# Fewer zero matmuls, an earlier first theta, sinks after the product, and one set of PSUM banks in a fused attention and mixer kernel

## The chip, the cores and the metric

The kernel runs on one core of one Trainium2 chip. The metric is the device time of one execution, in microseconds (us). Before the change three runs took 607.32, 607.62 and 608.21 us; the median is 607.62.

## The reference

The program is one fused block for batch 2, 768 positions and 512 channels, all in float32:

```
a   = softmax(where(is_sink | in_window, q k^T / 8, -1e9)) v   # 8 heads of 64, 4 sinks, window 128
x   = a as (2, 768, 512)
th  = x @ w_theta                                              # (512, 512)
y   = w_tok_r @ (x * cos th) + w_tok_i @ (x * sin th)          # mixes the 768 positions
u   = x + y;  x2 = u + relu(u @ w_ch)
m   = x2 + real(fft2(x2));  out = m + relu(norm(m) @ w_ch1) @ w_ch2
```

The kernel multiplies in a reduced float32 format and regains the precision by splitting an operand into a high and a low part: a product is three matmuls, high x high weight, high x low weight, low x high weight.

## The kernel before

The attention loop (`attn_banded`) walks through 12 tiles (n = 0 to 11, six of 128 positions for each of two batches), each in four steps s; 48 steps, and some more in which the rest drains. In the even steps `score_mms` issues a group of four score matmuls (one for each head) into the four banks of a ring, VectorE (L515) masks each and takes its minimum, and ScalarE (L519) takes the exponential; the second group of a tile fills the banks in reverse order. "S(n, 0)" and "S(n, 1)" below are the two score groups of tile n; S(2, 1), for one, belongs to step 10. One step later `turn` transposes the exponentials (`tp`), and ScalarE or VectorE copies them out. Six steps after a tile's first step `av` multiplies them with v into the one bank `oa`; the next step transposes the result back (`av_turn`), and VectorE normalizes it (L610 in the profile).

The 16 sink columns have their own product: `psk` is transposed into `oa`, copied to `pst`, and `av_sink` multiplies it with `vs` as the first writer of the accumulation in `oa`. `theta_gen` transposes the normalized tile (`tp<-ident,t`), splits it (ScalarE copies it to xT, GpSimd makes the high part, L808, and the low part, L211), and issues 12 matmuls into the bank `th` in the order high, high, low for each quarter of the channels.

The theta of tile u starts at step `first(u)` = 4u + 5 + max(4, 12 - u): step 17 for u = 0, 20 for u = 1, and 4u + 9 from u = 8 on. In steps 1 to 16 two matmuls of a tile of zeros go to the bank `th` after each step's scores (L651); they compute nothing that is used. The weights of theta come as 64-bit numbers and are converted on ScalarE and VectorE (`pump`, L279 to L291) in the steps of `THS`, and split one step later (L206, L211).

After attention `rest` runs `y_gen(0)`, the mixing over positions: for each block j of 128 positions the cosine and the sine product (`trig_mul`, L842 in the profile) are split and multiplied with converted weights into six banks: 24 matmuls of 512 columns and 24 of 256. j = 0 to 5 follow each other; cosine first, sine second, about 4.2 us of TensorE each.

Order: Tile's scheduler places the instructions of each engine by their dependencies and its own time model, so the code's order is only one input. The PSUM banks are eight tiles. One (`bank`) is held for the whole program; the other seven come from a pool of the attention part (`psa`), and after its end again seven from a second pool (`ps`) for the same memory. Every engine works its own queue in order.

## Time and profile before

| | us |
|---|---|
| median of three runs | 607.62 |
| profiled execution | 607.02 |
| its span, first to last instruction | 605.2 |
| TensorE (PE) busy | 588.4 |
| ScalarE (ACT), VectorE (DVE), GpSimd (POOL) busy | 345.4, 335.2, 332.8 |

The span is 1.8 us shorter than the profiled execution, and that execution is 0.6 us below the median. In a timeline row the columns are start, duration, engine, line, operation, out<-in and count; square brackets hold the idle time before and what ended it. Matmuls overlap, so a group's cost on TensorE is the distance from its start to the start of the next, not its duration. A float32 matmul of zeros or scores stands in the trace as two records.

### The profile page before, as it was taken

The page shows a single profiled execution, that of the slowest core. Times are in us where ns is not written, and L with a number is a line of the kernel's source. Part 1 is how long each engine was busy: PE and PEld are TensorE (multiplying, and loading weights), DVE is VectorE, ACT ScalarE, POOL GpSimd, SP SyncE. Part 2 cuts the span into 40 slices and gives each one's busy share as a digit, 9 for nine tenths or more (in the row PEclk, how much of TensorE's full clock was granted, in tenths as well). Part 3 has the DMA queues.
Part 4 walks back from the last instruction along what each step waited for, and adds up shares of the span by engine and source line. Part 5 has one row for each costly group of instructions (what it writes and reads, how often), then busy time and mean ns, then how long its engine had stood idle before and what let it go on. Part 6 is the DMA issues. An engine that isn't in the chain of part 4 may idle for free.

```text
span 605.2 us, 9829 instructions
## 1 busy us (share of the span) xinstructions
PE 588.4 (97%) x3606; PEld 513.1 (85%) x3606; DVE 335.2 (55%) x685; ACT 345.4 (57%) x774; POOL 332.8 (55%) x281
## 2 busy tenths in 40 slices
PE   8999999998999999989999999999999999999995
PEld 6777777786888899968999999998998899998994
DVE  5767657756999678983566765465334211121112
ACT  5776666667774564556678784437447444344340
POOL 1113664658885552517654746759757565665650
PEclk9999999999999999999999999999999999999998
DMA  7942333310334323710067650100001000010001
GB/s 227 343 137 67 110 122 105 89 36 0 105 106 137 116 70 105 209 35 2 2 179 206 195 152 0 53 2 0 2 0 54 1 0 1 2 52 1 0 2 58
DMA packets 23338, 46.63 MB, mean 77 GB/s; under 512 B 2512, under 2 KB 9552, under 8 KB 23280
## 3 DMA queue, kind: packets, MB, share of 16 engines
q1 hardware_dynamic: 22032, 43.74, 23.2%
q0 software_dynamic: 1248, 2.17, 1.2%
q8 instruction: 30, 0.49, 0.3%
q14 instruction: 28, 0.23, 0.1%
HBM read 42.75 MB, written 3.15 MB: 76 GB/s over the span
## 4 chain that ended last, share of the span: by engine, by line
PE 83%; DVE 8%; ACT 5%; issue 1%; POOL 1%; DMA 0%; ACTq 0%; DVEq 0%; POOLq 0%
PE pc L221 26%; PE acc L221 22%; PE s L221 9%; PE bank L221 8%; PE oa L221 3%; PE th L221 3%; PE tp L226 3%; PE sc L221 2%; PE th L651 2%; PE s L226 2%; ACT p L519 1%; ACT t L206 1%; POOL t L211 1%; PE bank L391 1%; DVE t L211 1%
## 5 line engine op out<-in xcount | busy, mean ns | idle before, releaser
L211 POOL TENSOR_TENSOR t<-t 128x512 fp32r<-128x512 f32 x151 | 202.7, 1363 | 166.9 <-ACT t L206 138.1
L221 PE MATMUL acc<-t 128*128 128x512 f32 x648 | 178.7, 394 | 0.0
L206 ACT ACTIVATE t<-t 128x512 fp32r<-128x512 f32 x172 | 102.1, 626 | 70.8 <-PE acc L221 26.5
L221 PEld LDWEIGHTS acc<-t 128*128 128x128 f32 x648 | 116.5, 188 | 17.9
L221 PE MATMUL pc<-t 128*128 128x384 f32 (+1 forms) x672 | 124.9, 314 | 1.0 <-POOL t L211 0.6
L221 PEld LDWEIGHTS pc<-t 128*128 128x128 f32 x672 | 113.8, 188 | 10.9 <-POOL t L211 0.8
L1156 DVE SCALAR_TENSOR_TENSOR t<-pc,t 128x384 fp32r<-128x384 f32 x64 | 35.6, 557 | 124.2 <-ACT t L1155 122.9
L221 PE MATMUL s<-t 128*128 128x256 f32 (+3 forms) x492 | 70.5, 286 | 1.6 <-DVE st L1076 0.8
L221 PE MATMUL pc<-uh,t 128*128 128x384 f32 x256 | 70.6, 337 | 0.0
L221 PEld LDWEIGHTS s<-t 128*128 128x128 f32 x492 | 65.9, 190 | 4.9 <-DVE st L1076 1.0
L211 POOL TENSOR_TENSOR t<-xT,t 128x512 fp32r<-128x512 f32 x39 | 52.8, 1372 | 28.2 <-ACT t L206 27.9
L1155 ACT ACTIVATE t<-pc 128x384 fp32r<-128x384 f32 x64 | 31.3, 489 | 60.8 <-PE pc L221 58.0
L221 PE MATMUL bank<-t 128*128 128x512 f32 x216 | 65.1, 398 | 0.9 <-DVE t L211 0.9
L279 ACT ACTIVATE raw<-raw 128x512 f32<-128x512 f32 x58 | 39.1, 678 | 14.8 <-DMA raw<-in_w_ch_dram 12.6
L221 PEld LDWEIGHTS pc<-uh,t 128*128 128x128 f32 x256 | 46.2, 188 | 0.8
L221 PEld LDWEIGHTS bank<-t 128*128 128x128 f32 x216 | 38.7, 188 | 7.8 <-DVE t L211 1.8
L221 PE MATMUL pc<-ul,t 128*128 128x384 f32 x128 | 43.0, 336 | 0.6 <-DVE ul L211 0.6
L519 ACT ACTIVATE p<-sc,nb 128x272 f32<-128x272 f32 (+1 forms) x72 | 32.8, 464 | 12.8 <-DVE nb L515 12.8
L221 PE MATMUL th<-t 128*128 128x512 f32 x132 | 35.9, 408 | 0.7 <-POOL t L211 0.7
L823 POOL TENSOR_SCALAR t<-t 128x512 f32<-128x512 f32 x12 | 25.4, 2117 | 16.2 <-ACT t L822 16.1
L515 DVE CUSTOM_DVE_ANT_0 sc<-sc,m 128x272 f32<-128x272 f32 (+1 forms) x72 | 28.6, 446 | 8.9 <-PE sc L221 8.9
L206 ACT ACTIVATE t<-xT 128x512 fp32r<-128x512 f32 x36 | 21.0, 625 | 19.1 <-PE acc L221 7.4
(144 smaller groups left out, 842.1 us busy)
## 6 DMA issues: line engine op xcount, KB each, us to landing
raw<-in_w_ch_dram SPq DMA_DIRECT2D x36, 512.0 KB, 3.8
kst<-in_k_dram SPq DMA_DIRECT2D x12, 256.0 KB, 4.1
t<-in_v_dram SPq DMA_DIRECT2D x12, 256.0 KB, 5.1
raw<-in_w_tok_rT_dram SPq DMA_DIRECT2D x6, 512.0 KB, 3.6
raw<-in_w_tok_iT_dram SPq DMA_DIRECT2D x6, 512.0 KB, 3.6
out_dram<-t SPq DMA_DIRECT2D x12, 256.0 KB, 2.1
t<-in_q_dram SPq DMA_DIRECT2D x11, 256.0 KB, 4.7
raw<-in_w_theta_dram SPq DMA_DIRECT2D x4, 512.0 KB, 6.9
```

Source lines behind the costliest of these rows:

```text
L206: return nc.scalar.activation(o, i, AF.Copy).ins
L211: e.tensor_tensor(o, x, hi.bitcast(F32), op=ALU.subtract)
L221: i = self.nc.tensor.matmul(o, lhsT=lhsT, rhs=rhs, start=start, stop=stop, skip_group_check=True).ins
L226: self.chained(self.nc.tensor.transpose(o, x, ident).ins)
L279: nc.scalar.activation(hf, hf, AF.Copy, scale=2.0 ** -112)
L391: nc.tensor.matmul(self.bank[:, 0:256], lhsT=z[:, 0:128], rhs=z, start=k == 0, stop=False, skip_group_check=True)
L515: nc.vector.tensor_tensor_reduce(out=sc[:, 0:wd], in0=sc[:, 0:wd], in1=mask, op0=ALU.add, op1=ALU.min, scale=-0.125, scalar=3.0e38, accum_ ...
L519: self.last_exp = nc.scalar.activation(p[:, h, 0:wd], sc[:, 0:wd], AF.Exp, bias=nb[:, h:h + 1], scale=-1.0, accum_out=sm[:, h:h + 1]).ins
L651: i = nc.tensor.matmul(self.zth[:, 0:256], lhsT=self.zz[:, 0:128], rhs=self.zz, start=s == 1, stop=False, skip_group_check=True,).ins
L823: nc.gpsimd.tensor_scalar(km, ph, MAGIC, MAGIC, op0=ALU.add, op1=ALU.subtract)
L1155: nc.scalar.activation(hh, hp, AF.Relu)
L1156: self.hl = nc.vector.scalar_tensor_tensor(hl, in0=hp, scalar=0.0, in1=hh.bitcast(F32), op0=ALU.max, op1=ALU.subtract).ins
```

## The change

The zeros stop after step 6 (`ZE`). `T0` falls from 12 to 10, which starts theta two steps earlier up to tile 6, and one for tile 7; two of the four theta weights are converted one and two steps earlier. In `theta_gen` the eight matmuls with the high part come first and the four with the low part last. The sink product is issued after the product with v and no longer opens the accumulation. The eight PSUM banks are allocated once, and the rings of both parts of the program name the same tiles.

```diff
@@ constants
-T0 = 12
+T0 = 10
+ZE = 7
-THS = (6, 9, 12, 15)
+THS = (6, 9, 11, 13)
@@ class _Ring
-    def __init__(self, pool, n, shape, dt, name, also=()):
-        self.tiles = [*also, *(pool.tile(shape, dt, name=f"{name}{i}") for i in range(n))]
+    def __init__(self, pool, n=0, shape=None, dt=None, name=None):
+        self.tiles = [pool.tile(shape, dt, name=f"{name}{i}") for i in range(n)] if n else pool
@@ start
-        self.bank = ctx.enter_context(tc.tile_pool(name="bank", bufs=1, space=PSUM)).tile([128, 512], F32, name="bank")
+        banks = ctx.enter_context(tc.tile_pool(name="bank", bufs=1, space=PSUM))
+        self.banks = [banks.tile([128, 512], F32, name=n) for n in ("bank", "a0", "a1", "a2", "c0", "c1", "s0", "s1")]
+        self.bank = self.banks[0]
@@ av_sink, av
-    def av_sink(self, n):
-        b, i = self.seq[n]
-        self.oacc = self.ps_acc.next().rearrange("p (a m) -> p a m", a=4)
-        if i < 2:
-            return
-        pst = self.pt.pop((n, 4))
-        for a in range(4):
-            self.mm(self.oacc[:, a], self.vs[b][:, 2 * a:2 * a + 2].rearrange("p h d -> p (h d)"), pst, a == 0, False)
-
     def av(self, n):
         b, i = self.seq[n]
-        acc = self.oacc
+        acc = self.ps_acc.next().rearrange("p (a m) -> p a m", a=4)
...
-                        i < 2 and hp == 0 and m == parts[0][1], hp == 3 and m == parts[-1][1],
+                        hp == 0 and m == parts[0][1], i < 2 and hp == 3 and m == parts[-1][1],
...
         self.hold = self.pe
+        if i >= 2:
+            pst = self.pt.pop((n, 4))
+            for a in range(4):
+                vs = self.vs[b][:, 2 * a:2 * a + 2].rearrange("p h d -> p (h d)")
+                self.mm(acc[:, a], vs, pst, False, a == 3)
@@ attn_banded
-            if 0 < s < first(0):
+            if 0 < s < ZE:
...
-            if 0 <= g + 1 <= last and k == 3:
-                self.av_sink(g + 1)
@@ theta_gen
-        for a in range(4):
-            wh, wl = self.ws["th", a]
-            self.mm(th, hi[:, a, :], wh, a == 0, False)
-            self.mm(th, hi[:, a, :], wl, False, False)
-            self.mm(th, lo[:, a, :], wh, False, a == 3)
-            if a < 3:
+        for k in range(12):
+            a, x = (k // 2, hi) if k < 8 else (k - 8, lo)
+            self.mm(th, x[:, a, :], self.ws["th", a][k < 8 and k % 2], k == 0, k == 11)
+            if k % 3 == 2 and k < 11:
                 yield
@@ all
-            self.ps_sc = _Ring(ps, 3, [128, 512], F32, "sc", [self.bank])
-            self.ps_tp = _Ring(ps, 2, [128, 512], F32, "tp")
-            self.ps_acc = _Ring(ps, 1, [128, 512], F32, "oa")
-            self.ps_th = _Ring(ps, 1, [128, 512], F32, "th")
+            self.ps_sc = _Ring(self.banks[0:4])
+            self.ps_tp = _Ring(self.banks[4:6])
+            self.ps_acc = _Ring(self.banks[6:7])
+            self.ps_th = _Ring(self.banks[7:8])
...
-            self.ps_acc = _Ring(ps, 3, [128, 512], F32, "acc", [self.bank])
-            self.ps_pc = _Ring(ps, 2, [128, 512], F32, "pc")
-            self.ps_s = _Ring(ps, 2, [128, 512], F32, "s")
+            self.ps_acc = _Ring(self.banks[0:4])
+            self.ps_pc = _Ring(self.banks[4:6])
+            self.ps_s = _Ring(self.banks[6:8])
```

So a0 to a2 are the old `sc` and `acc`, c0 and c1 the old `tp` and `pc`, s0 the old `oa`, s1 the old `th` (numbers 68 to 74 in the rows below). The engines' orders differ from the first dropped zeros up to block j = 2 of `y_gen(0)`; after that TensorE's is the same but for the names.

First place, TensorE from the second score group of tile 3 on; `<-kst,t` are scores, `<-ident,p` transposes of exponentials, `psk` that of the sinks, `<-t 64x128` the product with v, `pst` that of the sinks, `<-z` the zeros, `<-ident,t` into c_72 the transposes of the first theta. Before:

```order
L221 MATMUL sc_205<-kst,t 128x288
L221 MATMUL sc_204<-kst,t 128x288
L221 MATMUL sc_203<-kst,t 128x288
L221 MATMUL bank<-kst,t 128x288
L221 MATMUL oa_208<-pst_171,t 128x128 x4
L221 MATMUL oa_208<-t 64x128 x16
L651 MATMUL th_209<-z 128x256 x2
L226 MATMUL tp_207<-ident,p_186 128x128 x4
L651 MATMUL th_209<-z 128x256 x2
L226 MATMUL tp_206<-ident,p_186 128x128 x4
```

And now:

```order
L222 MATMUL a_70<-kst,t 128x288
L222 MATMUL a_69<-kst,t 128x288
L222 MATMUL a_68<-kst,t 128x288
L222 MATMUL bank<-kst,t 128x288
L227 MATMUL c_72<-ident,p_190 128x128 x2
L227 MATMUL s_73<-ident,psk_173 128x128
L227 MATMUL c_71<-ident,p_190 128x128 x4
L227 MATMUL c_72<-ident,t 128x128
L222 MATMUL s_73<-t 64x128 x16
L222 MATMUL s_73<-pst_175,t 128x128 x4
L227 MATMUL c_72<-ident,t 128x128 x3
```

The zeros are gone, the sinks stand behind the product, and the first theta's transposes have come in two steps earlier; with the zeros gone, transposes that stood ahead of the scores stand behind them.

Second place, TensorE where the mixing begins; `bank`, `acc`, `pc` (now `bank`, a_68 to a_70, c_71, c_72) with 128x512 and 128x256 are products of j = 0, `th` (now s_74) those of theta. Before, from the transposes of tile 10's result:

```order
L226 MATMUL oa_208<-ident,t 128x128 x4
L221 MATMUL bank<-t 128x512 x6
L226 MATMUL oa_208<-ident,psk_170 128x128
L226 MATMUL tp_206<-ident,t 128x128 x4
L221 MATMUL oa_208<-pst_172,t 128x128 x4
L221 MATMUL oa_208<-t 64x128 x16
L221 MATMUL th_209<-t 128x512 x12
L226 MATMUL oa_208<-ident,t 128x128 x4
L221 MATMUL pc_1675<-t 128x256 x3
L221 MATMUL acc_1672<-t 128x512 x3
L221 MATMUL pc_1675<-t 128x256 x3
L226 MATMUL s_1677<-ident,t 128x128 x4
```

And now, from the nineteenth product of j = 0 on (18 stand ahead of these rows, behind the transposes of tile 10's result):

```order
L222 MATMUL bank<-t 128x512 x3
L222 MATMUL a_68<-t 128x512 x3
L227 MATMUL s_73<-ident,psk_174 128x128
L227 MATMUL c_71<-ident,t 128x128 x4
L222 MATMUL a_69<-t 128x512 x3
L222 MATMUL c_72<-t 128x256 x3
L222 MATMUL a_70<-t 128x512 x3
L222 MATMUL c_72<-t 128x256 x3
L222 MATMUL s_73<-t 64x128 x16
L222 MATMUL s_73<-pst_176,t 128x128 x4
L222 MATMUL s_74<-t 128x512 x12
L222 MATMUL c_71<-t 128x256 x10
```

Before, six products stood ahead of the last tile's sinks and v product and 42 behind; now 36 stand ahead and 12 behind, and theta's last but one run of 12 stands behind the 36.

Third place, VectorE in the same stretch; L610 (now L609) normalizes the last tile out of `oa` (now s_73), L287, L288, L291 (now L288, L289, L292) convert weights, L842 (now L837) are the cosine and sine products, L211 (now L212) low parts. Before, from the last two conversion steps ahead of it:

```order
L291 SCALAR_TENSOR_TENSOR t<-raw_109,t 128x512
L291 SCALAR_TENSOR_TENSOR t<-raw_110,t 128x512
L610 TENSOR_TENSOR t<-oa_208,rs_180 128x512
L287 TENSOR_SCALAR t<-raw_108 128x512
L288 SCALAR_TENSOR_TENSOR t<-raw_108,t 128x512
L291 SCALAR_TENSOR_TENSOR t<-raw_108,t 128x512
L211 TENSOR_TENSOR t<-xT_71,t 128x512
L211 TENSOR_TENSOR t<-t 128x512
L842 TENSOR_TENSOR t<-t 128x512
```

And now:

```order
L292 SCALAR_TENSOR_TENSOR t<-raw_116,t 128x512
L292 SCALAR_TENSOR_TENSOR t<-raw_117,t 128x512
L609 TENSOR_TENSOR t<-s_73,rs_184 128x512
L212 TENSOR_TENSOR t<-t 128x512
L837 TENSOR_TENSOR t<-t 128x512
L288 TENSOR_SCALAR t<-raw_115 128x512
L289 SCALAR_TENSOR_TENSOR t<-raw_115,t 128x512
L292 SCALAR_TENSOR_TENSOR t<-raw_115,t 128x512
L837 TENSOR_TENSOR t<-t 128x512 x2
L212 TENSOR_TENSOR t<-xT_78,t 128x512
```

The normalization keeps its place in VectorE's row, with the conversions that stood ahead of it still ahead; behind it low parts and sine and cosine products have moved in front of conversions.

## Rows read from the trace of the kernel before

**Rows 1.** The page: engines' busy time, and the chain that ended last by engine.
```profile
PE 588.4 (97%) x3606; PEld 513.1 (85%) x3606; DVE 335.2 (55%) x685; ACT 345.4 (57%) x774; POOL 332.8 (55%) x281
...
PE 83%; DVE 8%; ACT 5%; issue 1%; POOL 1%; DMA 0%; ACTq 0%; DVEq 0%; POOLq 0%
```

**Rows 2.** Windows: each engine's busy time, granted clock (PEclk), DMA.
```profile
core 0: us, PE busy (x) PEld busy (x) DVE busy (x) ACT busy (x) POOL busy (x), PEclk, DMA share, GB/s
...
20.32:30.49 10.17, 10.17 (x86) 8.19 (x85) 8.70 (x27) 7.81 (x24) 1.98 (x3) 1.00 0.95 313
30.49:42.78 12.29, 12.29 (x94) 9.47 (x93) 8.31 (x25) 8.75 (x25) 2.42 (x3) 1.00 0.38 118
...
142.95:157.00 14.05, 11.68 (x83) 9.04 (x83) 12.27 (x18) 6.74 (x13) 10.15 (x6) 1.00 0.06 17
...
155.94:185.50 29.56, 29.43 (x166) 25.64 (x167) 28.94 (x34) 22.64 (x41) 24.68 (x17) 1.00 0.35 109
```

**Rows 3.** Zeros: their records from 18.9 us on, and a pair in TensorE's timeline.
```profile
L651 PE MATMUL th<-z x40: 379/379/483, 18.9 to 45.9; 128*128 128x256 f32 x40
...
18.92 1.03 PE L651 MATMUL th<-z 128*128 128x256 f32 x4
19.79 0.60 PE L226 MATMUL tp<-ident,p 128*128 128x128 f32 x4
```

**Rows 4.** Timeline, first score chains under the zeros: TensorE, ScalarE, VectorE.
```profile
24.67 0.95 PE L221 MATMUL sc<-kst,t 64*128 64x272 f32 x5
...
24.21 0.68 ACT L279 ACTIVATE raw<-raw 128x512 f32<-128x512 f32 x1
...
35.81 0.27 ACT L206 ACTIVATE pst<-oa 128x128 f32<-128x128 f32 x1
...
21.11 0.68 DVE L291 SCALAR_TENSOR_TENSOR t<-raw,t 128x512 int32<-128x512 int32 x1
21.71 0.44 DVE L515 CUSTOM_DVE_ANT_0 bank<-bank,m 128x272 f32<-128x272 f32 x1
```

**Rows 5.** TensorE's timeline: a theta that waits, S(11, 1), and the mixing's start.
```profile
61.65 2.56 PE L221 MATMUL th<-t 128*128 128x512 f32 x10 [0.73 <-POOL t L211]
...
131.33 0.95 PE L221 MATMUL sc<-kst,t 64*128 64x272 f32 x5 [0.28 <-ACT p L519]
...
142.95 0.73 PE L221 MATMUL bank<-t 128*128 128x512 f32 x2
144.56 1.52 PE L221 MATMUL bank<-t 128*128 128x512 f32 x4 [0.87 <-DVE t L211]
146.86 0.30 PE L226 MATMUL oa<-ident,psk 128*128 128x128 f32 x1 [0.79 <-DVE t L610]
...
153.41 0.60 PE L226 MATMUL oa<-ident,t 128*128 128x128 f32 x4
...
156.07 0.66 PE L226 MATMUL s<-ident,t 128*128 128x128 f32 x4 [0.66 <-DVE t L610]
```

**Rows 6.** ScalarE's timeline: end of the last exponentials, and the sine table.
```profile
134.46 0.21 ACT L519 ACTIVATION_READ_ACCUMULATOR p<-bank,nb 128x1 f32 x1
...
136.18 1.28 ACT L833 ACT_TABLE_LOAD   x1
```

**Rows 7.** VectorE, TensorE and GpSimd where blocks j = 2 and 3 are made.
```profile
155.34 0.68 DVE L610 TENSOR_TENSOR t<-oa,rs 128x512 f32<-128x512 f32 x1
...
184.82 0.68 DVE L211 TENSOR_TENSOR t<-t 128x512 fp32r<-128x512 f32 x1
...
173.31 0.86 PE L221 MATMUL bank<-t 128*128 128x512 f32 x3
...
154.30 2.90 POOL L823 TENSOR_SCALAR t<-t 128x512 f32<-128x512 f32 x1 [3.71 <-ACT t L822]
```

**Rows 8.** The page: loads of k, KB each, median us to landing.
```profile
kst<-in_k_dram SPq DMA_DIRECT2D x12, 256.0 KB, 4.1
```

**Rows 9.** The first zeros of the program, min/median/max ns of a weight load.
```profile
L391 PEld LDWEIGHTS bank<-z x14: 190/318/337, 1.3 to 5.6; 128*128 128x128 f32 x14
```

More of the change, by code (lines that the diff above doesn't have):

```diff
@@ L1192, in all @@
             e = ctx.enter_context(tc.tile_pool(name="e1", bufs=1, reuse_waits="tile"))
-            ps = ctx.enter_context(tc.tile_pool(name="psa", bufs=1, space=PSUM, reuse_waits="tile"))
             self.open_attention(e, banded)
-            self.ps_sc = _Ring(ps, 3, [128, 512], F32, "sc", [self.bank])
-            self.ps_tp = _Ring(ps, 2, [128, 512], F32, "tp")
-            self.ps_acc = _Ring(ps, 1, [128, 512], F32, "oa")
-            self.ps_th = _Ring(ps, 1, [128, 512], F32, "th")
+            self.ps_sc = _Ring(self.banks[0:4])
+            self.ps_tp = _Ring(self.banks[4:6])
+            self.ps_acc = _Ring(self.banks[6:7])
+            self.ps_th = _Ring(self.banks[7:8])
             if banded:
@@ L1204, in all @@
             e = ctx.enter_context(tc.tile_pool(name="e2", bufs=1, reuse_waits="tile"))
-            ps = ctx.enter_context(tc.tile_pool(name="ps", bufs=1, space=PSUM, reuse_waits="tile"))
-            self.ps_acc = _Ring(ps, 3, [128, 512], F32, "acc", [self.bank])
-            self.ps_pc = _Ring(ps, 2, [128, 512], F32, "pc")
-            self.ps_s = _Ring(ps, 2, [128, 512], F32, "s")
+            self.ps_acc = _Ring(self.banks[0:4])
+            self.ps_pc = _Ring(self.banks[4:6])
+            self.ps_s = _Ring(self.banks[6:8])
             self.bs = _Ring(e, 2, [128, 256], F32, "bs")
```

## The prediction

> **What bounds the kernel now.** I read the page first: TensorE is busy 588.4 of 605.2 us, and 83% of the chain that ended last lies on it [rows 1]. A microsecond taken off its queue counts if nothing else is late there. The windows say where that holds [rows 2]: from 20.32 to 42.78 us, the scores of tiles 2 and 3, TensorE has no idle time at all (10.17 and 12.29 us in full), but part of what it does is zeros. From 142.95 to 157.00, where attention ends and the mixing begins, it idles 2.37 us. From 155.94 to 185.50 VectorE is busy 28.94 of 29.56 us and GpSimd 24.68: what TensorE eats there comes out of two nearly full queues. The change touches these three places; by the orders, TensorE's work behind them is untouched.
>
> **The change part by part.** Times are those of the profiled execution (607.02 us: the span and 1.8 us around it); "lead" is how much earlier a point comes than in it.
>
> *Zeros.* 40 records are traced from 18.9 us on, which are 20 matmuls in ten pairs [rows 3]; all go. A pair of two matmuls, four records, costs the distance to the next start, 19.79 - 18.92 = 0.87 us. Ten make 8.7 us of TensorE's queue.
>
> *What the zeros covered.* Eight of the pairs, 7.0 us, lie between 20.32 and 42.78. Without them TensorE needs 22.46 - 7.0 = 15.5 us there, but VectorE is busy 8.70 + 8.31 = 17.0 us and ScalarE 16.6 [rows 2]. So at least 17.0 - 15.5 = 1.5 us come back as waits. The other bound is 7.0: each score group fills all four banks, the next waits for its last exponential, and if that chain is as long as today's distance between groups, nothing is won in this stretch. Between these I walked the new orders with today's durations. S(2, 0) could go 0.9 us earlier, but VectorE's first mask of it stands behind a weight's conversion that ends at 21.71, whatever TensorE does; the exponentials end at 24.2 as today (ScalarE's next work starts at 24.21), and S(2, 1) comes at 24.2 instead of 24.67 [rows 4]. TensorE has by then nothing else for 2.1 us. The second gap lies before tile 2's product with v: it writes the bank that `pst` is copied from, that copy stands behind three exponentials, and I get TensorE free at 35.1 and the product at 36.4 (today's copy starts at 35.81 [rows 4]): 1.3 us. The other groups come out without a gap. I take 2.1 + 1.3 = 3.4 us. The conversions of theta's weights, one and two steps earlier, are in this walk; their number is the same.
>
> *Low parts last.* At 61.65 ten theta matmuls wait 0.73 us for GpSimd's low part [rows 5]. Eight high products now stand in front, six more than today, at about 0.24 us each (the row's ten take 2.56 with the last one's drain): 1.4 us of cover against 0.73. I count 0.7; the bounds are 0 and 0.73.
>
> *Sinks behind the product.* The same matmuls in another order. Today the sinks wait for the `pst` copy, now the product does, since it opens the same bank; that wait is in the 3.4. Elsewhere I cost it at nothing, because other matmuls stand between copy and use. Without that cover it is the 0.27 us of a copy [rows 4] in each of eight tiles, 2 us.
>
> *Theta two steps earlier.* Moves work, removes none. At S(11, 1) ten more theta matmuls are done than today, 2.4 us. On SyncE's queue one k load moves ahead of three weight loads; k lands in 4.1 us [rows 8] and is needed six steps after its slot is free, so nothing waits for it.
>
> So S(11, 1), at 131.33 today [rows 5], comes at 131.33 - (8.7 - 3.4 + 0.7) + 2.4 = 127.7; in finished work the lead is 6.0.
>
> *The mixing's start.* It needs the last exponentials (they end 134.46 - 131.33 = 3.1 us after S(11, 1), plus 0.2), then on ScalarE two copies of a theta, one weight, the table load of 1.28 us [rows 6], and seven more operations of half a microsecond: 7.5 us. That gives 127.7 + 3.3 + 7.5 = 138.5 against 142.95 today [rows 5]: lead 4.4. TensorE gets there 1.6 us before (its queue from S(11, 1) is today's 142.95 - 131.33 = 11.6 us without the ten theta matmuls, 9.2). From there on the shared banks count: 36 products instead of six stand ahead of the last tile, so the waits of 0.87, 0.79 and 0.66 us [rows 5], 2.3 in all, are covered. Lead 6.7 by TensorE alone. Bounds: 0 if the cover fails, 2.37, all the idle time of the window.
>
> *What is late next.* Block j = 2 starts at 173.31 today [rows 7]; by TensorE alone it would start at 166.6. But its operands are made on VectorE behind the last tile's normalization (L610, at 155.34 today). That now waits for TensorE's transposes of tile 11, which stand behind nearly all of j = 0 (two halves of 4.2) and behind the sinks, v product and theta that take today's 146.86 to 153.41, 6.55 us [rows 5]: 138.5 + 8.3 + 6.5 = 153.3, against 153.41 today. They hardly come earlier. With their own 0.5 us and L610's 0.6 it ends at 154.4 against 156.0, a lead of only 1.6. Behind it j = 2 needs 17 VectorE operations and one ScalarE operation (0.6). Today the 32 operations from L610's end to the low part at 184.82 + 0.68 take 29.5 us, 0.92 each [rows 7]; undisturbed they follow each other in 0.60 (the mask starts 21.71 - 21.11 after a conversion [rows 4]). The difference is GpSimd working beside them. Today GpSimd stands 3.71 us behind a theta [rows 7]; two of its operations now come before that wait and fall out of the stretch. The 17 GpSimd operations in it [rows 2] bring 32 x 0.32 = 10.2 us, two of them 1.2, so I take 0.92 - 0.04 = 0.88. Then j = 2 starts at 154.4 + 17 x 0.88 + 0.6 = 170.0: lead 3.3. Bounds: 0.60 gives 165.2, but TensorE comes at 166.6 (lead 6.7); the other end is full exclusion, all of GpSimd's busy time on top of VectorE's 0.60, which is rival 4 (a loss of 5.0). I stay near today's price because the same operations meet there.
>
> The Trainium skill, page SBUF — State Buffer, section "Who interferes with whom", speaks against the change here: a VectorE instruction with two SBUF inputs and a GpSimd instruction exclude each other for a whole instruction. By that rule 32 x 0.60 us and 24.68 us of GpSimd would need 43.9 us. The trace does not agree as it stands: both fitted into 29.56 us with 28.94 and 24.68 busy [rows 2]. What the rule would give is the last rival.
>
> Behind j = 3 TensorE's order is that of before, and I let the lead of 3.3 stay to the end: 607.02 - 3.3 = 603.7. The median of the runs lies 0.6 above the profiled execution: 604.3.
>
> **The rivals.**
> (1) *VectorE's price is no limit.* If its operations cost 0.75 or less, j = 2 starts with 5.5 to 6.7 us of lead, and with a first gap that closes too (2.1) up to 8.8: 598.8 to 602.1. For it: GpSimd idles before 154.30 and can take work forward. Against: 28.94 of 29.56.
> (2) *The lead is spent.* At 1.01 to 1.15 us per operation, within 1.2 us of today's 173.31 is where j = 2 starts: 606.4 to 608.8. For it: the normalization's lead of 1.6 is small. Against: that price is above today's 0.92. Then the change does not do what it says: zeros are off the queue, and it waits as long.
> (3) *The clock falls.* Without zeros TensorE works 15.5 of 15.5 + 3.4 us in the stretch of tiles 2 and 3, 82%. In the window from 142.95 it worked 11.68 of 14.05, 83%, at a granted clock of 1.00 (2.4 GHz) [rows 2]; that is against it. At the lower level (1.2 GHz) a price is the first zeros, 318 ns for a weight load against 190 at best [rows 9]: 15.5 x 0.67 = 10.4 us longer, less the 3.4 of gaps: 604.3 + 7.0 = 611.3. The Trainium skill, page TensorE: Matmul & The Clock Gate, "Part 4: PE-mode transpose", says that transposes do not count as activity for the clock in the way matmuls do, and much of what is left between the scores is transposes; by that rule this rival would be the forecast, and the trace of before, where zeros always stand beside, cannot refute it for this stretch.
> (4) *Slower at j = 2.* VectorE and GpSimd exclude each other. The place is the stretch behind L610; the price is (32 x 0.60 + 24.68) / 32 = 1.37 per operation. Then j = 2 starts at 154.4 + 23.3 + 0.6 = 178.3, 5.0 later than today: 612.6. It decides from 1.15 per operation on. Against it: today's 0.92.
>
> **How the numbers follow.** Forecast, 1.2 to 5.5 us won (602.1 to 606.4): 0.54. Rival 1: 0.24; rival 2: 0.13; rival 3: 0.04; rival 4: 0.05. A measurement here can tell 0.2%, 1.2 us, from no change. Faster is forecast and rival 1, 0.78; same is rival 2, 0.13; slower is 3 and 4, 0.09. The range 600.0 to 607.2 leaves out the lower part of rival 1 (0.07), the upper part of rival 2 (0.05), and 3 and 4.
>
> **What would show it.** Right: the zeros end before 19 us; S(3, 0) at about 29 instead of 30.49 and S(4, 0) near 40 instead of 42.78, with 2 to 4 us of TensorE waits from 20 to 40 and a granted clock of 1.00; first product of j = 0 near 138.5 and no TensorE idle from there to 160; then TensorE waiting for ScalarE or VectorE ahead of j = 2, some 3 us. Wrong: no wait ahead of j = 2 (rival 1); long waits for exponentials from 20 to 60 (rival 2); PEclk under 1.00 (rival 3); VectorE operations beyond 1.15 us behind L609 (rival 4).

## The result, and the profile after

The changed kernel takes 612.88 us (median of 6 executions, 611.92 to 615.80) against 607.68 us before: a ratio of 1.0095, 95% interval 1.0069 to 1.0122, some 5 us slower where 3.3 us faster was forecast. The profiled executions differ by 610.8 - 605.2 = 5.6 us of span. The page after, busy time and chain, against [rows 1]:

```profile
PE 579.7 (95%) x3566; PEld 505.8 (83%) x3566; DVE 335.7 (55%) x685; ACT 345.0 (56%) x774; POOL 329.6 (54%) x281
...
PE 77%; DVE 11%; ACT 7%; issue 2%; DMA 1%; POOL 1%; ACTq 0%; SPq 0%; DVEq 0%; POOLq 0%
```

TensorE does 8.7 us less, as worked out for the zeros, and its share of the chain falls from 83% to 77%. So it waits more, and the windows say where. Columns are those of [rows 2]; first before, cut at new places, then after:

```profile
0.00:43.00 43.00, 41.36 (x289) 32.22 (x291) 28.48 (x114) 28.47 (x92) 6.43 (x12) 1.00 0.71 236
43.00:143.00 100.00, 97.00 (x747) 74.54 (x745) 66.48 (x202) 68.06 (x201) 54.60 (x47) 1.00 0.29 85
143.00:170.00 27.00, 24.63 (x155) 20.25 (x155) 24.63 (x30) 18.25 (x34) 22.66 (x15) 1.00 0.19 60
170.00:177.00 7.00, 7.00 (x42) 6.13 (x42) 7.00 (x8) 5.49 (x11) 6.42 (x4) 1.00 0.44 147
177.00:185.00 8.00, 8.00 (x48) 6.97 (x47) 8.00 (x13) 5.36 (x10) 4.63 (x3) 1.00 0.21 67
```

```profile
0.00:43.00 43.00, 36.48 (x261) 26.60 (x263) 28.42 (x114) 29.40 (x94) 8.01 (x13) 1.00 0.73 236
43.00:143.00 100.00, 92.71 (x738) 71.91 (x735) 70.74 (x204) 66.22 (x199) 54.90 (x46) 1.00 0.28 85
143.00:170.00 27.00, 26.89 (x173) 22.78 (x171) 17.80 (x23) 16.04 (x30) 18.47 (x14) 1.00 0.18 59
170.00:177.00 7.00, 0.00 (x0) 0.00 (x0) 6.75 (x11) 5.01 (x11) 3.00 (x2) 0.75 0.12 37
177.00:185.00 8.00, 7.93 (x37) 6.80 (x38) 7.79 (x13) 6.36 (x12) 6.25 (x5) 0.79 0.49 165
```

Idle time of TensorE is the length less its busy time. Up to 43 us it goes from 1.64 to 6.52, from 43 to 143 us from 3.00 to 7.29: together 9.2 us more, which eats the 8.7 of zeros. From 143 to 170 us it goes from 2.37 to 0.11: the one set of banks covers what the prediction said. But VectorE, busy for 24.63 of these 27 us before, is now idle for 27 - 17.80 = 9.2 us of them, and from 170 to 177 us TensorE does nothing, its granted clock falls, and in the eight us behind that it is 0.79 in the mean, between its levels of 1.2 and 2.4 GHz.

The places by name. TensorE's timeline after: two waits in attention, S(11, 1), the first product of j = 0, the transposes ahead of the last normalization, theta of tile 11 and block j = 2 ([rows 5, 7] are their like before).

```profile
78.60 1.97 PE L222 MATMUL s<-t 128*64 128x128 f32 x32 [1.48 <-ACT pst L207]
91.20 0.95 PE L222 MATMUL a<-kst,t 64*128 64x272 f32 x5 [1.41 <-ACT p L522]
131.42 0.95 PE L222 MATMUL a<-kst,t 64*128 64x272 f32 x5
142.61 0.73 PE L222 MATMUL bank<-t 128*128 128x512 f32 x2 [1.37 <-ACT t L207]
157.20 0.60 PE L227 MATMUL s<-ident,t 128*128 128x128 f32 x4
166.71 3.18 PE L222 MATMUL s<-t 128*128 128x512 f32 x12
177.07 1.22 PE L222 MATMUL bank<-t 128*128 128x512 f32 x2 [7.18 <-ACT t L207]
```

VectorE, ScalarE and SyncE's queue on the way to j = 2:

```profile
147.90 0.29 DVE L208 COPY pst<-s 128x128 f32<-128x128 f32 x1 [4.02 <-PE s L227]
157.90 0.69 DVE L609 TENSOR_TENSOR t<-s,rs 128x512 f32<-128x512 f32 x1 [2.86 <-PE s L227]
169.63 1.29 DVE L837 TENSOR_TENSOR t<-t 128x512 f32<-128x512 f32 x2 [0.99 <-ACT t L830]
174.61 1.75 DVE L837 TENSOR_TENSOR t<-t 128x512 f32<-128x512 f32 x1
```
```profile
168.32 0.67 ACT L280 ACTIVATE raw<-raw 128x512 f32<-128x512 f32 x1 [4.24 <-DMA raw<-in_w_tok_iT_dram]
176.39 0.63 ACT L207 ACTIVATE t<-t 128x512 fp32r<-128x512 f32 x1 [1.99 <-DVE t L837]
```
```profile
155.50 9.53 SPq L256 DMA_DIRECT2D raw<-in_w_tok_iT_dram  x2
```

VectorE waits twice for TensorE, 4.02 and 2.86 us, because sinks and transposes now stand behind products of j = 0. The last normalization starts at 157.90 instead of 155.34 [rows 7]. The cosine half of tile 2 is the 17th operation behind it and ends at 174.61 + 1.75 = 176.36; ScalarE rounds it, and j = 2 starts at 177.07, 3.8 us later than before. On the way ScalarE stood 4.24 us at a weight that had not landed: SyncE could issue that load only when VectorE had freed its buffer, and sines and cosines stood behind the weight. The lower clock adds 8 x (1 - 0.79) = 1.7 us. 3.8 + 1.7 = 5.5 of the 5.6 us.

### The profile page after: what moved, and what is told of

Same layout as the page of the kernel before. It is cut to its first block, busy times and chain, and to the rows that moved or that the text cites. A ratio compares the mean times of both kernels' runs of the same rounds, so it can differ in the third digit from the quotient of the medians.

```text
span 610.8 us, 9742 instructions
## 1 busy us (share of the span) xinstructions
PE 579.7 (95%) x3566; PEld 505.8 (83%) x3566; DVE 335.7 (55%) x685; ACT 345.0 (56%) x774; POOL 329.6 (54%) x281
## 4 chain that ended last, share of the span: by engine, by line
PE 77%; DVE 11%; ACT 7%; issue 2%; DMA 1%; POOL 1%; ACTq 0%; SPq 0%; DVEq 0%; POOLq 0%
PE c L222 25%; PE a L222 23%; PE s L222 15%; PE bank L222 8%; ACT p L522 2%; PE s L227 2%; PE c L227 2%; ACT t L207 2%; DVE a L518 1%; DVE t L289 1%; PE bank L394 1%; DVE t L292 1%; DVE t L288 1%; DVE t L208 1%; ACT raw L280 1%
## 5 line engine op out<-in xcount | busy, mean ns | idle before, releaser
L212 POOL TENSOR_TENSOR t<-t 128x512 fp32r<-128x512 f32 x151 | 201.1, 1351 | 167.2 <-ACT t L207 139.0
L222 PE MATMUL a<-t 128*128 128x512 f32 x648 | 179.5, 396 | 0.0
L222 PE MATMUL s<-t 128*128 128x256 f32 (+3 forms) x976 | 128.8, 299 | 4.6 <-ACT pst L207 2.3
L222 PEld LDWEIGHTS a<-t 128*128 128x128 f32 x648 | 117.3, 189 | 18.3
L222 PE MATMUL c<-t 128*128 128x384 f32 (+1 forms) x672 | 125.8, 315 | 1.1 <-POOL t L212 0.6
L222 PEld LDWEIGHTS c<-t 128*128 128x128 f32 x672 | 114.4, 189 | 11.0 <-POOL t L212 0.8
L222 PEld LDWEIGHTS s<-t 128*128 128x128 f32 (+1 forms) x976 | 107.8, 171 | 16.8 <-ACT pst L207 3.3
L1151 DVE SCALAR_TENSOR_TENSOR t<-c,t 128x384 fp32r<-128x384 f32 x64 | 35.6, 556 | 123.1 <-ACT t L1150 121.8
L222 PE MATMUL c<-uh,t 128*128 128x384 f32 x256 | 70.6, 337 | 0.0
L212 POOL TENSOR_TENSOR t<-xT,t 128x512 fp32r<-128x512 f32 x39 | 52.6, 1366 | 28.5 <-ACT t L207 28.2
L280 ACT ACTIVATE raw<-raw 128x512 f32<-128x512 f32 x58 | 39.1, 677 | 18.9 <-DMA raw<-in_w_ch_dram 13.5
L222 PEld LDWEIGHTS c<-uh,t 128*128 128x128 f32 x256 | 46.2, 188 | 0.8
L222 PE MATMUL c<-ul,t 128*128 128x384 f32 x128 | 43.1, 336 | 0.6 <-DVE ul L212 0.6
L818 POOL TENSOR_SCALAR t<-t 128x512 f32<-128x512 f32 x12 | 24.6, 2048 | 14.6 <-ACT t L817 10.9
```

The costliest lines, as they stand in the source:

```text
L212: e.tensor_tensor(o, x, hi.bitcast(F32), op=ALU.subtract)
L222: i = self.nc.tensor.matmul(o, lhsT=lhsT, rhs=rhs, start=start, stop=stop, skip_group_check=True).ins
L280: nc.scalar.activation(hf, hf, AF.Copy, scale=2.0 ** -112)
L818: nc.gpsimd.tensor_scalar(km, ph, MAGIC, MAGIC, op0=ALU.add, op1=ALU.subtract)
L1151: self.hl = nc.vector.scalar_tensor_tensor(hl, in0=hp, scalar=0.0, in1=hh.bitcast(F32), op0=ALU.max, op1=ALU.subtract).ins
```

## The experiments

The ratios are to runs of the kernel before on the same chip, with 95% intervals. The medians of that kernel lie between 607.4 and 607.9 us in these sets, so a difference of half a microsecond between two experiments on different chips tells nothing.

### The one set of banks and block j = 2

**Banks alone**, on the kernel before: the four rings take `self.banks[0:4]`, `[4:6]`, `[6:7]`, `[7:8]`, then `[0:4]`, `[4:6]`, `[6:8]`, as in the change; nothing else.

> The kernel before with the one set of banks alone; zeros, theta, sinks and low parts as before. Theory (the banks): the shared banks let the scheduler put 36 products of j=0 ahead of the last AV block and ten more ahead of the last tile's transposes, so those and theta of tile 11 come later, and the trig of tile 2 falls behind that of tiles 3 and 7 in VectorE's queue. TensorE then waits 6 to 8 us ahead of block j=2, its clock falls there, and the time is that of the changed kernel, 611 to 613 us. Rival (the wait ahead of j=2 comes from the changed attention, by which the last tile's transposes are late): no such wait, the idle 2.3 us between the first product and j=2 is covered, 605.4 us.

612.86 us, 1.0092 (1.0075 to 1.0109): the changed kernel's time, with attention as before. Its windows, the transposes of the last tile, the normalization and j = 2:

```profile
143.00:170.00 27.00, 25.73 (x173) 22.18 (x171) 20.46 (x25) 17.39 (x33) 21.78 (x16) 1.00 0.18 59
170.00:177.00 7.00, 2.60 (x10) 1.80 (x10) 6.97 (x11) 4.32 (x9) 3.08 (x2) 1.00 0.00 0
177.00:185.00 8.00, 7.29 (x33) 6.24 (x34) 7.89 (x12) 6.24 (x11) 5.04 (x5) 0.79 0.63 200
```
```profile
158.59 0.60 PE L226 MATMUL s<-ident,t 128*128 128x128 f32 x4
159.29 0.69 DVE L612 TENSOR_TENSOR t<-s,rs 128x512 f32<-128x512 f32 x1 [2.51 <-PE s L226]
```
```profile
177.71 1.22 PE L221 MATMUL bank<-t 128*128 128x512 f32 x2 [4.81 <-ACT t L206]
```

The normalization is 4 us late by the banks alone, and the wait ahead of j = 2 with its clock is there (4.81 us, with 1.57 more in theta of tile 11 just before, against the 6 to 8 expected). The rival falls.

**Old PSUM tiles** in the changed kernel (the inverse edit).

> The changed kernel with the two old sets of PSUM tiles back; all else as changed. Theory (the banks): VectorE's order after the last normalization is that of before (tile 2's products first), no wait of more than 1.5 us ahead of j=2, clock 1.00 there; what is left is attention without the zeros, whose idle of TensorE up to 143 us stays near 13.8 us against 4.6 before, so 606.3 to 607.7 us. Rival (the wait comes from the changed attention): it stays slower, 610 to 613 us. Rival 2 (the prediction's sum for the zeros holds as soon as the banks are as before): 602 to 604 us.

610.14 us, 1.0062 (1.0040 to 1.0084): the time lies in the first rival's range, but not for its reason. The wait ahead of j = 2 is gone, as the theory said, but another came that I had not thought of:

```profile
PE s L227 <- DVE t L607: 4.1, 1, 4.1
```

Theta's transposes of tile 11 wait 4.1 us for the normalized tile, where before it was 0.66 [rows 5]; with the banks shared, products stand between. So a part taken out of the change can bring a new wait elsewhere.

**Tile 2's products first**, in the changed kernel:

```
 if n == 0:
+    self.trig_tile(0, 2, "v")
+    tm = self.tm
     ...                          # theta of tile 11
-if u == 0 and j + 2 < NS:
+if u == 0 and 0 < j < NS - 2:
```

> The changed kernel with one step moved: the sine, cosine and products of tile 2 are written ahead of theta of tile 11 instead of behind it, so that VectorE multiplies them before the last normalization. Theory (the order of tile 2's products behind the last normalization makes the wait): TensorE goes from theta of tile 11 to j=2 without a wait of more than 1 us, its clock stays at 1.00, and 7.2 us of wait and some 1.7 us at the low clock go: 603.7 us (603 to 605). Rival (VectorE has too much to do in this stretch, whatever the order): the wait moves to j=3 or later, 608 to 612 us.

605.34 us, 0.9968 (0.9955 to 0.9982): 7.5 us faster than the changed kernel by moving one step in the order. The wait and the low clock there are gone. It falls 1.6 us short of the gain expected (603.7 us): a wait of 1.2 us for VectorE stands at 186.9 now, and in the profiled execution the clock fell near 26 and 36 us (rows further below).

**The wait filled with zeros**, in the changed kernel: `for _ in range(16)` a matmul of `self.zz` on `p0[0][:, 0:256]` ahead of j = 2.

> The changed kernel with 16 matmuls on zeros more (128x256, added to a bank of the product, which they leave as it is), written between blocks j=1 and j=2, where TensorE waits 7.2 us. They take 16 x 0.43 = 6.9 us, so j=2 still starts near 177 us. Theory (the wait also costs the clock: 0.75 granted in 170 to 177 us and 0.79 in the eight that follow, where eight us of work at full clock would take 8 x 0.79 = 6.3): granted clock 1.00 from 165 to 185 us and 612.9 - 1.7 = 611.2 us. Rival (the clock's loss there is small against the zeros that run past the wait): 612.9 us or more.

610.72 us, 1.0050 (1.0037 to 1.0063). Fourteen of the sixteen matmuls stand in the wait, two ahead of theta of tile 11. TensorE's j = 2 starts at 177.12 as before the edit, now at full clock:

```profile
170.00:177.00 7.00, 6.55 (x31) 5.39 (x29) 6.74 (x11) 5.01 (x11) 2.96 (x2) 1.00 0.14 36
177.00:185.00 8.00, 7.88 (x44) 6.90 (x45) 6.96 (x11) 5.61 (x12) 5.59 (x5) 1.00 0.52 168
```

So some 2 us of the loss were the clock behind the wait (2.2 by the medians, 610.8 - 609.2 = 1.6 by the spans of the profiled executions), and work that computes nothing bought them back.

**The last tile's transposes ahead**, in the changed kernel:

```
 for dd in range(4):
+    if not b and not j and c:
+        self.hold = getattr(self, "turned", None)  # set in av_turn, behind its last transpose
     big(dd)
     ...
+    if not b and not j and c:
+        self.hold = getattr(self, "turned", None)
     small(dd)
```

> The changed kernel, with the second half of j=0's products (c = 1) held behind the transposes of the last tile: 24 products stand ahead of these instead of 46; the one set of banks and all else stays. Theory (VectorE starves behind the late transposes): 22 products of some 0.175 us go behind them, the last normalization starts near 154 us instead of 157.90, the wait ahead of j=2 shrinks by about that, from 7.2 to some 3 us, and the clock's loss with it: 612.9 - 3.9 - 1.0 = 608.0 us (607 to 609). Rival (VectorE's price per operation makes the wait): 612 to 613 us.

609.14 us, 1.0021 (1.0003 to 1.0039). The normalization starts 3.4 us sooner, and the time falls by 3.7 instead of the theory's 4.9, just above its range and far from the rival's 612 to 613.

```profile
154.54 0.67 DVE L610 TENSOR_TENSOR t<-s,rs 128x512 f32<-128x512 f32 x1
```

The profiled execution was one of three, of ten, at a mean granted clock of 0.999; these took 605.8 to 606.7 us, the others, at 0.987 to 0.995, 608.1 to 611.2. In the profile j = 2 starts at 170.24, and the longest wait in it is 2.13 us. So with the banks still shared the loss goes, at full clock, once this order is put right: what cost here is the order that the banks let in.

### Attention without the zeros

**Zeros alone**, on the kernel before: `if 0 < s < 7` for `if 0 < s < first(0)`.

> The kernel before with the zeros ended at the sixth step, and nothing else. Theory (the zeros covered waits all through the first part of attention): TensorE's idle up to 143 us goes from 4.6 to 11 to 14 us and eats the 8.7 us of zeros, 606 to 608 us. Rival (the idle of the changed kernel comes from the moved theta, sinks and low parts): idle goes up by about 3.4 us only, and the time is 607.7 - 8.7 + 3.4 = 602.4 us, or 604 if TensorE's lead is spent in part at block j=2.

604.37 us, 0.9948 (0.9931 to 0.9964), the rival's second number. TensorE's idle time goes from 1.64 to 5.35 and from 3.00 to 3.19 us, 3.9 in all:

```profile
0.00:43.00 43.00, 37.65 (x268) 27.42 (x268) 30.12 (x121) 29.23 (x95) 6.63 (x12) 1.00 0.71 238
43.00:143.00 100.00, 96.81 (x731) 74.09 (x731) 67.79 (x199) 68.73 (x201) 57.09 (x48) 0.98 0.27 85
```

The prediction's 3.4 for this was nearly right; the rest of what went wrong in attention lies in the other three edits. Four runs start from the kernel with tile 2's products first (605.34 us).

**Sinks first again** (`av_sink` back, one step ahead of `av`):

> As the kernel with tile 2's products first (605.34 us), with the sinks written ahead of the AV products again. Theory (the sinks behind the products cost most of what zeros, theta, sinks and low parts together lost between 43 and 143 us, by TensorE's waits for the sink's copy, 2.3 us in two waits against 0.9 before): the waits for pst fall to 0.9 us or less and the time to 603.3 to 604.0 us. Rival (theta two steps sooner is the cause, by ScalarE's exponentials that come late behind the weights of theta): no change, 605.0 to 605.7 us.

605.53 us, 0.9961 (0.9948 to 0.9974): no change, by a path of its own. The longest wait for `pst` falls from 1.5 to 0.8 us, and idle from 43 to 143 us from 7.35 to 4.41 us, but in the profiled execution the clock was 0.52 and 0.62 in the eight us from 34, and one execution at a mean clock of 0.998 took 603.2.

**Theta later again** (`T0 = 12`, `THS = (6, 9, 12, 15)`):

> As the kernel with tile 2's products first (605.34 us), with theta and its weights at the old steps (T0 12, weights at 6, 9, 12, 15). Theory (sinks): waits for pst stay 2.3 us, the waits for the exponentials near 62 and 91 us stay, 605.0 to 605.7 us. Rival (theta): the two waits for the exponentials of 0.8 and 1.4 us fall to 0.4 each and the time to 603.5 to 604.3 us.

602.94 us, 0.9925 (0.9897 to 0.9953): the rival, and by its median the fastest kernel of all, 4.9 us under the kernel before. No score group waits longer than 0.5 us for exponentials now, where one waited 1.4, and idle from 43 to 143 us is 3.13 instead of 7.35:

```profile
0.00:43.00 43.00, 38.01 (x271) 27.67 (x271) 30.92 (x123) 30.24 (x99) 6.61 (x12) 1.00 0.74 241
43.00:143.00 100.00, 96.87 (x736) 74.89 (x737) 67.06 (x197) 67.96 (x197) 56.74 (x48) 0.98 0.27 83
```
```profile
184.82 0.85 PE L222 MATMUL c<-t 128*128 128x256 f32 x5 [2.24 <-DVE t L212]
```

**Low parts between again** (the loop over `a` of before in theta):

> As the kernel with tile 2's products first (605.34 us), with theta's low parts between the others again. Theory (low parts last save nothing that matters, since the wait of 0.7 us that they remove came once): 605.3 to 606.1 us. Rival (low parts last shift the groups of three and cost): 604.0 to 605.0 us.

609.60 us, 1.0023 (1.0002 to 1.0044), beyond the theory's end: low parts last gain more than I gave them, here with the clock in it. Four executions at a mean clock of 0.997 to 0.998 took 607.0 to 607.9, the others, at 0.986 to 0.995, 609.5 to 613.1; with the low parts last, the one execution at 0.997 took 605.0.

**All three as before**, with zeros ended, shared banks and tile 2 first:

> The kernel before with the zeros ended at the sixth step, the one set of banks and tile 2's products ahead of theta of tile 11; theta, sinks and low parts as before. Theory (these three cost 3 to 4 us of the changed kernel, and the banks with the right order of tile 2 gain): 601.3 to 602.6 us, the idle of TensorE between 43 and 143 us near 3.2 us and none above 1 us between 143 and 185 us. Rival (the banks' cover is spent later, where VectorE has the same work to do): 604.0 to 604.8 us, as with the zeros ended alone.

603.77 us, 0.9942 (0.9923 to 0.9961): near the rival's numbers. Against the zeros ended alone, the banks with the order mended gain 0.6 us, which these runs can't tell from nothing.

**Theta sooner on zeros alone**, and **sinks and low parts on zeros alone**, both in the old banks:

> The kernel before with the zeros ended at the sixth step (604.37 us) and theta and its weights two steps sooner, nothing else. Theory (theta sooner does the harm by itself, 2.4 us by the comparison 605.34 against 602.94): 606.3 to 607.3 us, TensorE's idle between 43 and 143 us 5 us or more against 3.2. Rival (harm only with the sinks behind and the low parts last): 604.0 to 605.0 us.

> The kernel before with the zeros ended at the sixth step (604.37 us), the sinks behind the products and the low parts last; theta and the two sets of PSUM tiles as before. Theory (these two gain a little, 0.8 us by 603.77 against 602.94): 603.2 to 604.2 us. Rival (they cost, in the old banks): 605.0 to 607.0 us.

605.54 us, 0.9959 (0.9945 to 0.9974), and 607.21 us, 0.9995 (0.9985 to 1.0004). The first lies between theory and rival; idle from 43 to 143 us is 3.6 us, so most of theta's harm in that stretch needs the other edits. The second lies just above the rival's range: theta's transposes of tile 11 wait 4.05 us for the normalization, as in the run with the old tiles. So the sinks or the low parts bring that wait; which of the two was not tried.

**Theta later and sinks first**, with low parts last, shared banks, tile 2 first:

> As the kernel with tile 2's products first and theta at the old steps (602.94 us), with the sinks ahead of the AV products too; zeros to the sixth step, low parts last, one set of banks. Theory (the sinks' place is worth nothing beyond 0.5 us): 602.4 to 603.4 us. Rival (at full clock the kernel with the sinks first and theta sooner took 603.2 against 605.0): 600.9 to 602.0 us.

609.63 us, 1.0027 (1.0016 to 1.0038), against both: idle from 43 to 143 us is 7.9 us, with waits of 2.3 and 1.9 us for `pst`. The edits do not add up. Here too the `pst` copies that TensorE waits for stand right behind exponentials in ScalarE's queue (at 59.95 and 110.23 us).

**Two more pairs of zeros**, on each of the two kernels with theta later:

> As the kernel with tile 2's products first and theta at the old steps (602.94 us), with two more pairs of zeros, at the seventh and eighth steps. Theory (where TensorE waits between 19 and 46 us its clock falls in some executions and a pair of zeros is worth more than its 0.87 us there): granted clock 1.00 or near it in all executions, 601.8 to 602.9 us, and the executions lie closer together. Rival (they delay TensorE by their own time): 603.8 to 604.7 us.

> As the run before it in this list (theta at the old steps, sinks first), with the two more pairs of zeros at the seventh and eighth steps. Theory (the zeros hold the clock through the waits): 0.5 to 1 us below it, with a smaller spread. Rival (they cost 0.9 to 1.7 us, as they take TensorE's time where it does not wait): above it by that.

603.76 us, 0.9933 (0.9920 to 0.9946), and 609.53 us, 1.0032 (1.0021 to 1.0044). The first is 0.8 us above the kernel without them, within the intervals; the second can't be told from it. A gain was not seen.

### What the banks are worth once the order is right

**Banks and tile 2 first**, on the kernel before:

> The kernel before with the one set of banks and tile 2's products ahead of theta of tile 11; zeros, theta, sinks and low parts as before. Theory (the banks cover 2.3 us of idle and the right order keeps it): 607.7 - 2.3 = 605.4 us. Rival (the cover is spent at j=3 and j=4, where VectorE's operations are late, as the waits of 1 to 2 us there in the kernels with this order show): 606.8 to 607.7 us.

609.50 us, 1.0030 (1.0012 to 1.0048), worse than both. From 143 to 170 us TensorE has no idle time, but VectorE has 4.7 us of it instead of 2.4, and two blocks later TensorE stands:

```profile
143.00:170.00 27.00, 27.00 (x180) 23.64 (x179) 22.31 (x27) 19.92 (x37) 20.36 (x16) 1.00 0.12 39
185.00:205.00 20.00, 16.88 (x88) 14.51 (x86) 16.56 (x21) 9.82 (x17) 12.33 (x11) 0.91 0.56 169
```
```profile
187.54 0.50 PE L221 MATMUL c<-t 128*128 128x256 f32 x2 [0.99 <-ACT t L206]
190.17 2.50 PE L221 MATMUL c<-t 128*128 128x256 f32 x10 [2.13 <-DVE t L211]
```

**Transposes ahead, with theta later and tile 2 first**, holding c = 1, and holding all but the first half of c = 0:

> The kernel with theta at the old steps and tile 2's products first (602.94 us), with the same hold: 24 products of j=0 ahead of the last tile's transposes instead of 47. Theory: the last normalization comes near 152 instead of 155.42 us, the wait of 2.2 us at 184.8 goes, 600.5 to 601.5 us. Rival (what TensorE gains at 184.8 it loses as uncovered waits between 140 and 155, where those products stood): 602.5 to 603.5 us.

> As the run before it in this list, with more held: of j=0 only the first half of c = 0 (12 products) stands ahead of the last tile's transposes. Theory (the balance lies between covering TensorE and feeding VectorE): VectorE gains another 2 us of lead that it no longer needs, TensorE idles some 1 to 2 us between 140 and 152, 601.0 to 602.5 us, that is not better than with 24 ahead. Rival (VectorE still bounds): 599.5 to 600.5 us.

605.86 us, 0.9973 (0.9963 to 0.9983), and 605.73 us, 0.9961 (0.9944 to 0.9977): both are above all four ranges and above the kernel without the hold. The wait at 184.8 went, as said, but theta of tile 11 now reaches TensorE before VectorE has made its low part. In the first a wait of 3.4 us, with a clock of 0.72 from 166 to 172 us, takes its place (2.5 us in the second):

```profile
167.33 2.07 PE L222 MATMUL s<-t 128*128 128x512 f32 x4 [3.44 <-DVE t L212]
```

## Why the prediction was wrong

Three terms of the sum failed, and together they are the whole miss: the lead that attention was to hand over (4.1 us short), the time of the 17 VectorE operations behind the last normalization (2.9 us too long), and the clock behind the wait, which was put at nothing (1.7 us). 604.3 + 4.1 + 2.9 + 1.7 = 613.0, and 612.9 was measured.

- *Zeros, 8.7 us off TensorE's queue.* Right: 588.4 to 579.7.
- *What the zeros covered, 3.4 us.* About right by the run without them alone (3.9); S(2, 1) came at 25.18, not 24.2.
- *Sinks and theta at nothing, low parts last at -0.7.* Sinks and theta are the step of attention that failed; low parts last was under-rated, if anything. I let "other matmuls stand between" hide the sinks' new wait and counted theta as moved work, "their number is the same".

The first loss is theta's. S(3, 0) came at 29.23 us, near the 29 said, but S(4, 0) at 42.35 instead of 40; with the zeros alone gone it came at 39.66. VectorE now converts a theta weight between the masks of S(3, 0), so ScalarE's exponentials stand:

```profile
31.47 1.41 DVE L292 SCALAR_TENSOR_TENSOR t<-raw,t 128x512 int32<-128x512 int32 x1
32.80 0.44 DVE L518 CUSTOM_DVE_ANT_0 a<-a,m 128x272 f32<-128x272 f32 x1
33.39 0.49 ACT L522 ACTIVATE p<-a,nb 128x272 f32<-128x272 f32 x1 [1.17 <-DVE nb L518]
```

In all eight profiles with theta and its weights sooner the first row of five records of S(3, 1) starts at 34.7 to 35.6 us, in all nine with the old steps and fewer zeros at 32.5 to 33.5; the kernel with tile 2 first (35.15) and the same with theta later (33.00) differ in nothing else. Work that moves in front of a chain costs the chain its time, though the number of operations is the same.

The second loss lies between 43 and 143 us, where the changed kernel idles 4.3 us more. On the kernel with tile 2 first, theta at its old steps gives 4.2 of them back, sinks at their old place 2.9. The row at 78.60 shows how the sinks' part arises: the whole product now waits for the `pst` copy, and on ScalarE that copy stood behind two exponentials that had waited 3.89 us for VectorE:

```profile
77.33 0.49 ACT L522 ACTIVATE p<-bank,nb 128x272 f32<-128x272 f32 x1 [3.89 <-DVE nb L518]
...
78.27 0.28 ACT L207 ACTIVATE pst<-s 128x128 f32<-128x128 f32 x1
```

How the edits combine in this second stretch stays open: they do not add up.
- *S(11, 1) at 127.7, first product at 138.5.* 131.42 and 142.61. The lead at the mixing's start was 0.3 instead of 4.4 us: the 4.1 above.
- *The banks cover 2.3 us.* Right (2.26), and it was no gain.
- *Block j = 2.* The place and the chain were right, the price of the chain was not. From the first product on, the sum gave 8.3 + 6.5 = 14.8 us to the last transposes, and it took 157.20 - 142.61 = 14.6. The 17 operations behind the normalization took 176.36 - 158.5 = 17.9 us, 1.05 each, not 0.88; 1.2 of the 2.9 us are VectorE's own waits, the longer for ScalarE behind the weight's load, a stall that I had not looked for. 4.1 us of lateness and 2.9 of length make 177.07 out of 170.0.
- *The price of VectorE's operations, 0.88 us each.* The prediction held both engines' busy times, 28.94 and 24.68 of 29.56 us [rows 2], against the rule that VectorE and GpSimd exclude each other. That reading was wrong: the record of an instruction that is held up runs on while it is held up, so such busy times can add up to more than the stretch. Laid side by side, the rows after show the two taking turns; the last row is one with GpSimd idle:

```profile
162.34 1.75 POOL L212 TENSOR_TENSOR t<-t 128x512 fp32r<-128x512 f32 x1
162.97 1.67 DVE L292 SCALAR_TENSOR_TENSOR t<-raw,t 128x512 int32<-128x512 int32 x1
164.06 1.74 POOL L819 TENSOR_TENSOR t<-t 128x512 f32<-128x512 f32 x1
167.96 0.68 DVE L212 TENSOR_TENSOR t<-xT,t 128x512 fp32r<-128x512 f32 x1
```

GpSimd ends at 164.09, VectorE 0.55 us later at 164.64, GpSimd 1.16 us after that at 165.80. In the whole trace after there are 90 places where a GpSimd TENSOR_TENSOR and a VectorE operation with two inputs, both in SBUF, overlap, each of 128x512: in 46 VectorE ends at least 0.53 us after GpSimd, in 44 at least 1.1 us before it, in none between. The trace of before has 86 such places, and they are alike; where a VectorE input lies in PSUM, most overlap freely. With GpSimd idle, VectorE's operations follow each other in 0.60 us. So the price is paid for each meeting, some 1.1 us, and not for each operation: six of the 17 met a GpSimd instruction and took 1.56 to 1.70 us to the next start, 6.3 us more than at 0.60. 17 x 0.60 + 6.3 + 1.2 of own waits = 17.7 of the 17.9 us; the forecast had 17 x 0.28 = 4.8 for the meetings and nothing for waits.
- *Rivals.* Rival 4 named the side, the place, nearly the time (178.3 for j = 2, 612.6 us) and, by these rows, the mechanism. The Trainium skill's rule behind it (SBUF — State Buffer, "Who interferes with whom") is borne out by the 176 places above. The rival's price, 1.37 us per operation, was too high, since it added all of GpSimd's busy time, held-up time included. It said that the mechanism decides from 1.15 on; 1.05, in rival 2's span, was enough, because the chain started late. That the rival's time came so near is luck: the 4.1 us of lateness, which it did not have, stand in for most of the price that it had too high. Rival 3 had the clock at another place; it fell in the wait ahead of j = 2, and filling that wait gave some 2 us. Its price rested on the first zeros, but no row shows the lower level there: the windows from 0 to 8 us read 1.00. Behind the wait two matmuls of 256 columns took 0.42 us (178.10 to 178.52), where three take 0.36 at full clock in the same block. In 19 to 43 us the profiled execution kept 1.00, but the run with tile 2 first, whose attention is the same, fell there:

```profile
26.00:30.00 4.00, 4.00 (x39) 3.83 (x40) 3.31 (x12) 3.84 (x13) 0.29 (x1) 0.65 0.81 240
34.00:38.00 4.00, 3.63 (x17) 2.03 (x17) 3.16 (x12) 4.00 (x14) 1.28 (x1) 0.71 0.40 128
```

- *The banks' price.* With attention as before, the banks cost all that the changed kernel loses (612.86 against 612.88 us), so fewer zeros and the three edits beside them, taken together, brought nothing on top of the banks. The sum set the lead of attention against the transposes that stand behind the products and found them level with today's, "they hardly come earlier"; what the banks cost without that lead it never said. On unchanged attention the transposes come 158.59 - 153.41 = 5.2 us later, and the kernel is 5.3 us slower. The queue behind them was full, 28.94 of 29.56 us [rows 2]: I read that row for the price of an operation, and not for what an idle microsecond of VectorE ahead of it costs.

## What to carry to other kernels

Filling a bottleneck engine's idle time with its own later work is no gain if that work stands ahead of a short piece that a second, nearly full engine waits for: look at what becomes of the second engine's idle time in that stretch. Busy times of two engines that add up to more than the stretch are no proof that the two work side by side: lay their rows beside each other. Where an edit removes filler, "hidden by other work" must be worked out again for every other edit with the filler gone. And parts of a change that share queues are to be run alone and together, since here one step's place was worth 7.5 us and the other parts did not add up.

## What the runs showed of the hardware

The granted clock can fall in some executions of a program and not in others. In ten executions of one kernel without the later zeros (low parts between) the mean granted clock went from 0.998 to 0.986, and the time from 607.0 to 613.1 us. The kernel before stayed at 0.997 to 0.999 and within 606.5 to 608.7; with nothing but its later zeros gone, four executions ran at 0.994 to 0.998. Sixteen matmuls on zeros, written for one wait, were worth some 2 us.

VectorE operations with both inputs in SBUF and GpSimd's TENSOR_TENSOR, both of 128x512, took turns instruction by instruction: a VectorE operation that was held up ended 0.55 us after the GpSimd instruction and took 1.67 to 1.78 us in the stretch above instead of 0.68, and its record shows the time held up as busy.
